# Attention before a mixture of experts: two key blocks of every pair weighted by split products in place of float32 ones, in a new order

## The chip, the cores and the metric

One core of one Trainium2 chip runs the whole kernel. The time is the device time of one execution in microseconds (us), the median of several runs. The engines are named as in the profile: PE (TensorE matmul), PEld (its weight loads), DVE (VectorE), ACT (ScalarE), POOL (GpSimd), SP (SyncE, which issues most DMAs).

## What is computed

Attention with 8 batches of 8 heads, 1152 keys of 64 values each, and queries that are averaged two by two; its output is the input of a layer of 8 experts with a fixed capacity.

```python
q_pool = q.reshape(B, H, S // 2, 2, D).mean(axis=3)            # 8, 8, 576, 64
scores = np.matmul(q_pool, k.transpose(0, 1, 3, 2)) / np.sqrt(D)
attn = np.exp(scores - np.max(scores, axis=-1, keepdims=True))
attn = attn / (np.sum(attn, axis=-1, keepdims=True) + 1e-09)
x = np.matmul(attn, v)                                         # to (4608, 512): one row a token
logits = x @ w_gate                                            # 8 experts
...                                                            # greedy routing, 576 tokens an expert
out[mask] = np.maximum(x[mask] @ w1[e], 0.0) @ w2[e]
```

## The kernel before

**Tiling.** The 64 heads are taken two at a time: 32 *pairs*, numbered 0 to 31. A pair has 18 *steps*, one for each head of the pair and each block of 128 keys (steps 0 to 8 the first head, 9 to 17 the second). A step holds 512 of a head's 576 queries; the 64 queries that are left of either head make the *shared block*, which both heads fill together.

**One step** (`step`, from line 847). PE forms the scores of 128 keys by 512 queries in one of three PSUM banks, by two matmuls of 512 columns (lines 841 and 842). ACT takes the exponential into the float32 tile P (line 858). The high part of P is its upper half, read in place as bfloat16; the low part PM = P - high, in float16, is made by a subtraction (line 863), on POOL, or on DVE for the steps listed in `AT["pd"]` (in pair 0 `AT["pd0"]`) and for two steps of the last pair that are fixed in the code. Then PE multiplies by the values (line 875), twelve matmuls a step: for each 128 queries high by top values, high by low values, low by top values, all added into the one PSUM bank `av`. A step that is listed in `AT["f32"]` is done otherwise: no PM is made, and P is multiplied as float32 by the values in float32 (line 872), which the chip runs as eight instructions a step:

```python
whole = g % NSTEP in AT["f32"]
if not whole:
    en, eng, dur = ("DVE", nc.vector, 600) if g % NSTEP in pd or (n == npair - 1 and g % 3 == 2 and kb > 5) else ("POOL", nc.gpsimd, 1000)
    od.add(g + 0.2, en, dur, lock=1, fn=lambda: eng.tensor_tensor(pm, p, hi, op=OP.subtract), ...)
...
if whole:
    nc.tensor.matmul(a, p[:, qs], VF[:, s, kb], start=False, stop=kb == NKB - 1, skip_group_check=True)
    continue
for y, (out, w, v) in enumerate(((a, hi, top), (a[:, :D], hi, low), (a, pm, top))):
    nc.tensor.matmul(out, w[:, qs], v, ...)
```

**The end of a pair.** The shared block's probabilities PJ are float32 in either kernel, and line 911 multiplies them by the float32 values into the same bank. After that DVE empties `av` (lines 921, 924, 925: RS and X). The products of the next pair cannot begin in `av` before that.

**Work for the next pair** goes on meanwhile: DMAs bring keys, queries and values; ACT and DVE split them into high and low parts (on DVE: KL line 647, QL line 637, the low part of V line 692; each reads two tensors of SBUF); PE forms score maxima in two PSUM banks `mt` (lines 749, 757, 766, 769), DVE reduces them (MX, line 742, then CM line 795), PE turns them (line 818), DVE writes AU (line 820) and frees the bank. Every second pair PE also turns X and forms gate logits (lines 938, 952; LS on DVE).

**Routing tables.** 32 small operations, 22 of DVE and 10 of POOL, build constants for the routing (`routing_tables`, DVE's at line 478). They form one chain, in which each writes what the next one needs.

**The order.** Nothing is scheduled at run time: each engine runs its own list in order. The class `Timed` gives every operation a time: the number of its pair times `PERIOD`, plus its entry in the table `TIME`, whose keys name the pair (0 to 3 by number, `e` and `o` even and odd ones, `y` and `z` the last two), the operation and its step. It then emits the operation with the least time among those whose producers have been emitted. `AT["grp"]` lists after which steps of a head the products that are waiting go out as one group. The experts' part has a planner of its own.

Of the kernel before, what the change touches and what calls it, by code (L numbers as in the profile page):

```python
# [162 lines left out]
class Timed(Order):  # L163
# [21 lines left out]
    def emit(self):  # L185
# [36 lines left out]
      3, "wu": 50, "pd": [], "wv": 65, "pd0": [3, 4, 8, 9, 10, 17], "sp": 0, "d1": 2.5, "cw1":  # L222
      0.5093, "grp": [2, 4, 6, 7, 8, 9],
      "jq": [9, 12, 15], "f32": [16, 17]}
PERIOD = 23600
TIME = {"0auga": 7741, "0augb": 12864, "0augta": 6209, "0augtb": -4893, "0av0a10a": 3692, "0av0a12a": 8723,
# [277 lines left out]
def attention(ctx, tc, top, kb, sx, kt, qt, v, wg, x_dram, L, npair=NPAIR):  # L504
    nc = tc.nc
    const = ctx.enter_context(tc.tile_pool(name="att_const", bufs=1))
    psum = ctx.enter_context(tc.tile_pool(name="att_psum", bufs=1, space=PSUM))
    od = Timed(TIME, PERIOD, npair)

# [1254 lines left out]
```

## Time and profile before

| | |
|---|---|
| runs, median (least to most) | 1263.47 us (1263.2 to 1264.06), 3 runs |
| profiled execution | 1262.77 us, span 1261.0 us, mean granted TensorE clock 0.981 |
| busy PE | 1204.0 us, 95% of the span |
| busy DVE | 942.8 us, 75% |
| busy ACT | 869.3 us, 69% |
| busy POOL | 848.8 us, 67% |

How to read it: attention takes some 763 us of the span, the experts the rest, and the shares are means over both. A matmul's duration in the rows reaches into the next one's, since PE is pipelined; what a matmul costs is read from the distance between starts. The profile's lines are those of the kernel before; in the changed kernel the same code stands three lines higher (872 there is 875 here, 908 there 911 here).

### The profile page before, as it was taken

What the parts mean: (1) busy time and instruction counts of PE and PEld (TensorE: products, weight loads), DVE (VectorE), ACT (ScalarE), POOL (GpSimd) and SP (SyncE); (2) the same over time, 40 slices, a digit from 0 to 9 for tenths busy, and PEclk for the clock granted to TensorE, in tenths of its full rate; (3) what the DMA queues carried; (4) which work ended last, traced back from release to release, by engine and by line L of the source; (5) the groups of instructions that cost most, each with busy time, mean ns of one, the idle gap of its engine ahead of it and who ended that gap; (6) DMA issues with size and microseconds to landing.
All of it is one profiled execution on the core that took longest, in us unless ns stands there. A gap on an engine that the chain in (4) does not pass through costs nothing.

```text
span 1261.0 us, 36741 instructions
## 1 busy us (share of the span) xinstructions
PE 1204.0 (95%) x14619; PEld 839.5 (67%) x14619; DVE 942.8 (75%) x2290; ACT 869.3 (69%) x1603; POOL 848.8 (67%) x882
## 2 busy tenths in 40 slices
PE   8899999999989999999999997799899999999998
PEld 4566666666656666666666675576667677777776
DVE  7898888988887988888898835888776777762320
ACT  6687887888867888888788661457456564667731
POOL 4577787778858768878777680366575756668641
PEclk7899999999989999999999998999899999999999
DMA  7565576566565475566556300432553335253411
GB/s 211 153 170 132 154 178 143 148 166 157 132 150 143 137 174 150 137 163 168 133 148 147 94 10 20 171 127 79 175 168 117 130 118 195 88 196 121 142 38 38
DMA packets 95690, 171.03 MB, mean 136 GB/s; under 512 B 17694, under 2 KB 54558, under 8 KB 93342
## 3 DMA queue, kind: packets, MB, share of 16 engines
q1 hardware_dynamic: 82574, 107.09, 31.8%
q0 software_dynamic: 12800, 61.58, 16.4%
q8 instruction: 115, 1.88, 0.7%
q14 instruction: 57, 0.47, 0.1%
q10 hardware_dynamic: 144, 0.02, 0.0%
HBM read 99.63 MB, written 18.87 MB: 94 GB/s over the span
## 4 chain that ended last, share of the span: by engine, by line
PE 72%; DVE 14%; issue 4%; ACT 3%; POOL 3%; DMA 2%; another core or an unknown queue 0%; SPq 0%; POOLq 0%; DVEq 0%; ACTq 0%
PE po L1681 12%; PE av L875 12%; PE ph L1651 9%; PE sc L841 6%; PE sc L842 6%; DVE MX L742 5%; PE mt L749 5%; PE av L872 5%; PE kb L841 4%; PE kb L842 3%; PE av L911 3%; DVE KL L647 2%; POOL W2L L1635 1%; PE mt L938 1%; PE mt L766 1%
## 5 line engine op out<-in xcount | busy, mean ns | idle before, releaser
L863 POOL TENSOR_TENSOR PM<-P 128x512 f16<-128x512 f32 x506 | 534.6, 1111 | 176.5 <-ACT P L858 173.7
L742 DVE TENSOR_REDUCE MX<-mt 128x2 f32<-128x1024 f32 (+2 forms) x341 | 373.5, 1133 | 42.8 <-PE mt L749 30.1
L858 ACT ACTIVATE P<-sc 128x512 f32<-128x512 f32 x384 | 221.2, 598 | 71.3 <-PE sc L842 61.8
L875 PEld LDWEIGHTS <-P 128*128 128x128 bf16 x4096 | 202.7, 99 | 49.4 <-issue 29.8
L875 PE MATMUL av<-V,P 128*128 128x65 f16 (+1 forms) x4096 | 216.4, 194 | 0.3 <-DVE V L692 0.3
L875 PE MATMUL av<-V,PM 128*128 128x65 f16 x2048 | 209.8, 196 | 0.0
L875 PEld LDWEIGHTS <-PM 128*128 128x128 f16 x2048 | 190.1, 98 | 0.5 <-issue 0.4
L841 PE MATMUL sc<-QA,KA 128*128 128x512 f16 (+1 forms) x768 | 178.5, 286 | 1.1 <-ACT P L858 0.9
L842 PE MATMUL sc<-QB,KB 66*128 66x64 f16 (+2 forms) x768 | 176.6, 286 | 0.0
L1681 PE MATMUL po<-W2H,HX 128*128 128x512 f32 x512 | 169.0, 405 | 0.4 <-DVE OT L1691 0.4
L1651 PE MATMUL ph<-Xh,W1h 128*128 128x320 f16 (+1 forms) x512 | 147.3, 288 | 2.5 <-ACT Xh L1513 1.5
L1651 PE MATMUL ph<-Xl,W1h 128*128 128x320 f16 (+1 forms) x512 | 147.5, 288 | 0.6 <-DVE Xl L1515 0.6
L1651 PE MATMUL ph<-Xh,W1l 128*128 128x320 f16 (+1 forms) x512 | 147.4, 288 | 0.5 <-issue 0.5
L841 PEld LDWEIGHTS <-KA 128*128 128x128 f16 x1152 | 97.7, 99 | 74.4 <-issue 33.6
L858 ACT ACTIVATE P<-kb 128x512 f32<-128x512 f32 x192 | 114.9, 599 | 41.0 <-PE kb L842 40.0
L1660 DVE SCALAR_TENSOR_TENSOR HX<-ph,HX 128x256 fp32r<-128x256 f32 x128 | 53.3, 419 | 102.2 <-ACT HX L1656 98.6
L1681 PE MATMUL po<-W2L,HX 128*128 128x512 f32 (+1 forms) x320 | 127.8, 399 | 0.0
L1635 POOL TENSOR_TENSOR W1l<-W,W1h 128x512 f16<-128x512 f32 x62 | 72.2, 1168 | 77.1 <-ACT W1h L1629 73.3
L1651 PEld LDWEIGHTS <-W1h 128*128 128x128 f16 x1024 | 99.1, 98 | 36.3 <-issue 10.9
L1656 ACT ACTIVATE HX<-ph 128x256 fp32r<-128x256 f32 (+1 forms) x128 | 51.7, 409 | 103.1 <-PE ph L1651 93.6
L842 PEld LDWEIGHTS <-KB 66*128 66x128 f16 (+1 forms) x1152 | 95.2, 98 | 39.0 <-issue 3.3
L1681 PEld LDWEIGHTS po<-W2H,HX 128*128 128x128 f32 x512 | 94.5, 190 | 17.3 <-DVE OT L1691 0.9
(272 smaller groups left out, 2338.8 us busy)
## 6 DMA issues: line engine op xcount, KB each, us to landing
KD<-in_kt_dram SPq DMA_DIRECT2D x64, 288.0 KB
VD<-in_v_dram SPq DMA_DIRECT2D x32, 576.0 KB
QA<-QH SPq DMA_DIRECT2D x128, 72.0 KB
KA<-KH SPq DMA_DIRECT2D x64, 144.0 KB
KB<-KH SPq DMA_DIRECT2D x64, 144.0 KB
KA<-KL SPq DMA_DIRECT2D x64, 144.0 KB
x_dram<-X SPq DMA_DIRECT2D x16, 576.0 KB
QS<-in_qt_dram SPq DMA_DIRECT2D x31, 288.0 KB
```

What stands on the lines that cost most here:

```text
L742: od.add(t, "DVE", d, lambda: nc.vector.tensor_reduce(dst, src, axis=AX.X, op=OP.max), r=[f"m{m}"], w=w, tag="mr", k=z)
L749: nc.tensor.matmul(mt[s][:, y], pairs[b][s], KH[i][h, ks], start=True, stop=True)
L841: nc.tensor.matmul(c, KA[i][:, s, ks], QA[i][:, s, qs], start=first, stop=False, skip_group_check=True)
L842: nc.tensor.matmul(c, KB[i][:kr, s, ks], QB[i][:kr, s, qs], start=False, stop=last, skip_group_check=True)
L858: od.add(g + 0.1, "ACT", 480, lambda: nc.scalar.activation(p, c, AF.Exp, scale=1.0 / UNIT), r=[ck], w=[("P32", g % NP)], tag="exp", k=g % ...
L863: od.add(g + 0.2, en, dur, lock=1, fn=lambda: eng.tensor_tensor(pm, p, hi, op=OP.subtract), r=[("P32", g % NP)], w=[("PM", g % NM)], tag=" ...
L872: nc.tensor.matmul(a, p[:, qs], VF[:, s, kb], start=False, stop=kb == NKB - 1, skip_group_check=True)
L875: nc.tensor.matmul(out, w[:, qs], v, start=kb == 0 and j == 0 and y == 0, stop=kb == NKB - 1 and y == 2, skip_group_check=True)
L1635: eng.tensor_tensor(o, a, b, op=OP.subtract), r=[key] + sr + [(nm + "H", z, y)], w=[(nm + "L", z, y)], first=first, lock=1, tag="wl" if nm ...
L1651: nc.tensor.matmul(p, a[:, d, fs], b[:, d, qs], start=z == 0, stop=z == 11)
L1660: V.scalar_tensor_tensor(HL[:, f, 64 + 256 * hf:320 + 256 * hf], p[:, :256], 0.0, h[:, :256], op0=OP.max, op1=OP.subtract)
L1681: nc.tensor.matmul(o[:n], a[:, z, q0:q0 + n], b[:, z], start=z == 0 and y == 0, stop=z == 7, skip_group_check=True)
```

## The change

The list `f32` becomes empty. Steps 16 and 17 of every pair are done like the others: twelve split matmuls each in place of the float32 ones, and a PM each. The list `pd` gets step 11, whose PM goes from POOL to DVE in pairs 1 to 31. With `grp` the products of a head's steps 6 and 7 go out together. The table `TIME` is new throughout; among its entries the 22 table operations of DVE get times that are 12980 apart.

```diff
-      3, "wu": 50, "pd": [], "wv": 65, "pd0": [3, 4, 8, 9, 10, 17], "sp": 0, "d1": 2.5, "cw1":
-      0.5093, "grp": [2, 4, 6, 7, 8, 9],
-      "jq": [9, 12, 15], "f32": [16, 17]}
+      3, "wu": 50, "pd": [11], "wv": 65, "pd0": [3, 4, 8, 9, 10, 17], "sp": 0, "d1": 2.5, "cw1":
+      0.5093, "grp": [2, 4, 6, 8, 9],
+      "jq": [9, 12, 15], "f32": []}
...
-        "2tablesj": -17424, "2tba": 8188, "2tbb": -15946, "2tbc": -18774, "2tbd": -24432, "2tbe": 311221, "2tbf":
+        "2tablesj": -20403, "2tba": 32600, "2tbb": 45580, "2tbc": 58560, "2tbd": 71540, "2tbe": 84520, "2tbf": 97500,
```

No other line differs, and in the experts' part every engine's list is the same as before. Over the whole kernel POOL makes 537 PMs (506 before) and DVE 39 (6 before).

**PE, the end of pair 20.** P and PM are step tiles, L872 and L911 before are the float32 products of the steps and of the shared block. Before, from the last split product on:

```order
L875 LDWEIGHTS P_134
L875 MATMUL av<-V_99,P_134 128x64
L875 LDWEIGHTS PM_145
L875 MATMUL av<-V_99,PM_145 128x65
L872 MATMUL av<-MS,P_135 128x65 x4
L872 MATMUL av<-MS,P_136 128x65 x4
L841 LDWEIGHTS KA_90
L841 MATMUL sc_153<-QA_94,KA_90 128x512
```

The change, the same place, up to the shared block (L872 is now the split product, L908 the shared block):

```order
L872 LDWEIGHTS PM_147
L872 MATMUL av<-V_99,PM_147 128x65
L872 LDWEIGHTS P_136
L872 MATMUL av<-V_99,P_136 128x65
L872 LDWEIGHTS P_136
L872 MATMUL av<-V_99,P_136 128x64
L872 LDWEIGHTS PM_147
L872 MATMUL av<-V_99,PM_147 128x65
L908 MATMUL av<-MS,PJ 64x65 x18
```

The float32 products of P are gone; the last product before the shared block now reads a PM.

**DVE, the routing tables.** Before, in pair 13's steps, 18 table operations (L478) stand in one piece ahead of AU; the last twelve rows of it:

```order
L478 TENSOR_SCALAR nib<-scratch 128x15 x4
L478 TENSOR_SCALAR nib<-scratch 128x16
L478 TENSOR_SCALAR scratch<-scratch 128x64
L478 TENSOR_SCALAR diag<-scratch 128x64
L478 TENSOR_TENSOR diag<-diag,scratch 128x64
L478 TENSOR_SCALAR scratch<-scratch 128x128
L478 TENSOR_SCALAR same_167<-scratch 128x128
L478 CAST slots<-scratch 128x640
L478 CAST slot_169<-scratch 128x5
L478 TENSOR_SCALAR jval<-scratch 128x36
L478 CAST TAB<-scratch 128x1 x2
L820 TENSOR_SCALAR AU<-mt_157 9x128
```

The change, DVE in one even pair (line 475 is the table operation):

```order
L634 SCALAR_TENSOR_TENSOR QL_88<-QS_119,KS_107,QH_86 128x576
L644 SCALAR_TENSOR_TENSOR KL_85<-KD_114,KS_107,KH_83 128x576
L675 TENSOR_SCALAR VE_125<-mt_156 128x1
L644 SCALAR_TENSOR_TENSOR KL_85<-KD_114,KS_107,KH_83 128x576
L739 TENSOR_REDUCE MX_128<-mt_156 128x2x4
L677 TENSOR_SCALAR VS_113<-VE_125 128x1
L681 TENSOR_SCALAR sx<-VS_113,sx 128x1
L739 TENSOR_REDUCE MX_128<-mt_157 128x2
L953 COPY LS<-mt_156 72x384
L475 TENSOR_TENSOR diag<-diag,scratch 128x64
```

The 22 table operations now stand alone, one or two to a pair, over a dozen pairs.

**DVE, after the first half of `av` is emptied** (X, 128x4x64), even pair. Before:

```order
L925 TENSOR_TENSOR X_104<-av,RS_149 128x4x64
L624 TENSOR_SCALAR KE_110<-KS_108 128x1
L626 TENSOR_SCALAR KE_110<-KS_108,KE_110 128x1
L628 TENSOR_SCALAR KS_108<-KE_110 128x1
L630 TENSOR_SCALAR KS_108<-KS_108 128x1
L742 TENSOR_REDUCE MX_127<-mt_157 128x2
L742 TENSOR_REDUCE MX_127<-mt_156 128x2
L692 SCALAR_TENSOR_TENSOR V_100<-VD_118,VS_113,V_100 128x9x64 x2
```

The change:

```order
L922 TENSOR_TENSOR X_105<-av,RS_149 128x4x64
L627 TENSOR_SCALAR KS_108<-KS_108 128x1
L860 TENSOR_TENSOR PM_141<-P_130 128x512
L689 SCALAR_TENSOR_TENSOR V_100<-VD_118,VS_113,V_100 128x9x64 x2
L739 TENSOR_REDUCE MX_127<-mt_156 128x2
L739 TENSOR_REDUCE MX_127<-mt_157 128x2
L644 SCALAR_TENSOR_TENSOR KL_85<-KD_115,KS_108,KH_84 128x576 x2
```

DVE now makes step 11's PM there, with both V parts straight behind it, and two KL follow after the next two reductions.

## Rows read from the trace of the kernel before

**Rows 1.** Spans: core, us, mean granted TensorE clock.
```profile
core 0: 1261.0 us, clock 0.981
```

**Rows 2.** Timeline, DVE: start us, us, form; start of emptying `av` at pair ends.
```profile
353.37 0.22 DVE L921 TENSOR_SCALAR RS<-av,VS 128x5 f32<-128x5 f32 x1 [2.36 <-PE av L911]
...
383.38 0.22 DVE L921 TENSOR_SCALAR RS<-av,VS 128x5 f32<-128x5 f32 x1
...
405.03 0.22 DVE L921 TENSOR_SCALAR RS<-av,VS 128x5 f32<-128x5 f32 x1 [2.35 <-PE av L911]
...
428.62 0.21 DVE L921 TENSOR_SCALAR RS<-av,VS 128x5 f32<-128x5 f32 x1
...
450.28 0.22 DVE L921 TENSOR_SCALAR RS<-av,VS 128x5 f32<-128x5 f32 x1 [2.36 <-PE av L911]
...
473.72 0.21 DVE L921 TENSOR_SCALAR RS<-av,VS 128x5 f32<-128x5 f32 x1
```

**Rows 3.** Windows: stretch, length, busy PE, PEld, DVE, ACT, POOL (count), clock, DMA.
```profile
366.00:384.00 18.00, 14.19 (x188) 9.94 (x185) 14.45 (x41) 9.30 (x19) 7.16 (x8) 0.81 0.42 102
372.00:374.00 2.00, 1.80 (x19) 0.97 (x19) 1.79 (x8) 0.52 (x1) 0.00 (x0) 0.50 0.04 9
428.60:473.70 45.10, 45.03 (x706) 29.73 (x705) 39.09 (x64) 37.34 (x68) 35.08 (x35) 1.00 0.62 158
722.00:763.00 41.00, 40.77 (x675) 29.29 (x671) 15.05 (x33) 25.01 (x46) 29.53 (x42) 1.00 0.09 24
```

**Rows 4.** Timeline, PE: a split step at 400.21, float32 steps, the shared block.
```profile
400.21 0.22 PE L875 MATMUL av<-V,P 128*128 128x65 f16 x2
...
400.58 0.38 PE L841 MATMUL sc<-QA,KA 128*128 128x512 f16 x1
...
401.88 1.90 PE L872 MATMUL av<-MS,P 128*128 128x65 f32 x16
403.71 1.27 PE L911 MATMUL av<-MS,PJ 128*64 128x65 f32 x36
```

**Rows 5.** Timeline, DVE and then PE, from the first to the last late table operation.
```profile
367.35 0.14 DVE L478 CAST pcole<-scratch 128x1 f32<-128x1 int32 x1
...
368.38 2.04 DVE L478 TENSOR_SCALAR nib<-scratch 128x15 f32<-128x15 int32 x5
...
371.88 0.27 DVE L820 TENSOR_SCALAR AU<-mt 9x128 f16<-9x128 f32 x1
...
372.20 1.01 PE L749 MATMUL mt<-KH,QH 64*128 64x512 f16 x3 [3.81 <-DVE AU L820]
```

**Rows 6.** Groups by form, two pairs (428.6 to 473.7): count, busy us, mean ns, idle before.
```profile
L647 DVE SCALAR_TENSOR_TENSOR KL<-KD,KS,KH 128x576 f16<-128x576 f32 x4 | 4.8, 1231 | 0.0
L692 DVE SCALAR_TENSOR_TENSOR V<-VD,VS,V 128x576 f16<-128x576 f32 x4 | 3.1, 809 | 0.0
L637 DVE SCALAR_TENSOR_TENSOR QL<-QS,KS,QH 128x576 f16<-128x576 f32 x2 | 1.6, 814 | 0.0
L863 POOL TENSOR_TENSOR PM<-P 128x512 f16<-128x512 f32 x33 | 34.7, 1109 | 10.2 <-ACT P L858 9.8
```

**Rows 7.** Timeline, POOL and DVE: five PMs while a KL runs; KL; five PMs alone.
```profile
430.36 5.55 POOL L863 TENSOR_TENSOR PM<-P 128x512 f16<-128x512 f32 x5
...
432.31 1.71 DVE L647 SCALAR_TENSOR_TENSOR KL<-KD,KS,KH 128x576 f16<-128x576 f32 x1
...
462.04 5.03 POOL L863 TENSOR_TENSOR PM<-P 128x512 f16<-128x512 f32 x5
...
469.46 0.81 DVE L647 SCALAR_TENSOR_TENSOR KL<-KD,KS,KH 128x576 f16<-128x576 f32 x1
```

**Rows 8.** Line 863: duration ns least/median/most, first and last start.
```profile
L863 DVE TENSOR_TENSOR PM<-P x6: 679/684/911, 29.3 to 746.8; 128x512 f16<-128x512 f32 x6
```

**Rows 9.** DMA that POOL issues: ns least/median/most.
```profile
L589 POOL DMA_DIRECT2D QS<-in_qt_dram x31: 836/883/1211, 14.2 to 682.8; - x31
```

More of the change, by code (lines that the diff above doesn't have):

```diff
@@ L221 @@
       -3.5, "cw": 0.5093, "fold0": 3.5, "fold1": 13.1, "aug": 13.9, "lag": 3, "np": 10, "nm": 9, "stick": 0.5, "nx":
-      3, "wu": 50, "pd": [], "wv": 65, "pd0": [3, 4, 8, 9, 10, 17], "sp": 0, "d1": 2.5, "cw1":
-      0.5093, "grp": [2, 4, 6, 7, 8, 9],
-      "jq": [9, 12, 15], "f32": [16, 17]}
+      3, "wu": 50, "pd": [11], "wv": 65, "pd0": [3, 4, 8, 9, 10, 17], "sp": 0, "d1": 2.5, "cw1":
+      0.5093, "grp": [2, 4, 6, 8, 9],
+      "jq": [9, 12, 15], "f32": []}
 PERIOD = 23600
-TIME = {"0auga": 7741, "0augb": 12864, "0augta": 6209, "0augtb": -4893, "0av0a10a": 3692, "0av0a12a": 8723,
[125 rows of a table removed]
-        "ekl1a": -26623, "eksa": -30018, "eksb": -103880, "eksc": -115231, "eksd": -117469, "elk0a": -136803, "elk1a":
[13 rows of a table removed]
-        -114263, "evsa": -1138, "evsb": -113652, "evsc": -114069, "evsd": -115770, "exa": -106982, "exb": -112457,
[6 rows of a table removed]
-        -137053, "ofolda": -137487, "ogba": 48053, "ogca": -132261, "ogcb": -129305, "ogla": 47500, "ogma": 46405,
-        "ogpa": -138552, "ogta": 43583, "ogtb": 44271, "ojaa": 38452, "oje0a": -132457, "oje1a": -133851, "oje2a":
-        -135820, "ojq0a": 17219, "ojq1a": 27290, "ojq2a": 33876, "okaa": -47428, "okh0a": -136159, "okh1a": -132399,
-        "okl0a": -31088, "okl1a": -36401, "oksa": -40537, "oksb": -136244, "oksc": -139976, "oksd": -138478, "olk0a":
[14 rows of a table removed]
-        -147762, "ovsd": 3810, "oxa": -128835, "oxb": -134705, "yauga": -318273, "yaugda": -330939, "yaugta": 6464,
[8 rows of a table removed]
-        "yksc": -302753, "yksd": -299894, "ylk0a": -326863, "ylk1a": -324184, "ylpa": -55508, "ylqa": -325577, "ylva":
[13 rows of a table removed]
-        -2194, "yvsb": -303618, "yvsc": -304154, "yvsd": 4358, "yxa": -304843, "yxb": -302503, "zauga": 4408,
[6 rows of a table removed]
-        "zexp9a": -324730, "zfolda": -320551, "zgca": -322303, "zgcb": -322620, "zgcc": -321911, "zgla": -328867,
-        "zglb": -328767, "zglc": -324813, "zgma": -189521, "zgmb": -347199, "zgmc": -348229, "zgta": -205694, "zgtb":
-        -350225, "zgtc": -348229, "zjaa": -176057, "zje0a": -323822, "zje1a": -322054, "zje2a": -326925, "zjq0a":
-        29263, "zjq1a": -216474, "zjq2a": -173800, "zkaa": -65924, "zkh0a": -322199, "zkh1a": -323089, "zkl0a":
-        -36141, "zkl1a": -36407, "zksa": -41417, "zksb": -325815, "zksc": -325806, "zksd": -326595, "zlk0a": -339282,
[14 rows of a table removed]
-        -327483, "zvsc": -331115, "zvsd": -328772, "zxa": -325966, "zxb": -328540}
@@ new lines @@
+TIME = {"0auga": 7900, "0augb": 19260, "0augta": 6495, "0augtb": 5547, "0av0a10a": 10554, "0av0a12a": 11649,
[123 rows of a table added]
+        "ekl1a": -24155, "eksa": -29474, "eksb": -112144, "eksc": -115548, "eksd": -118916, "elk0a": -141449, "elk1a":
[13 rows of a table added]
+        "evl1a": 13524, "evsa": 1884, "evsb": -1627, "evsc": -113184, "evsd": -110115, "exa": 30484, "exb": 38513,
[6 rows of a table added]
+        -156706, "ogca": -73450, "ogcb": -117226, "ogla": 48291, "ogma": 47154, "ogpa": -142314, "ogta": 43792,
+        "ogtb": 44448, "ojaa": 38944, "oje0a": -145530, "oje1a": -136541, "oje2a": -137525, "ojq0a": 16489, "ojq1a":
+        26294, "ojq2a": 33002, "okaa": -43084, "okh0a": -138482, "okh1a": -37150, "okl0a": -34150, "okl1a": -34218,
+        "oksa": -92933, "oksb": -40369, "oksc": -137671, "oksd": -38474, "olk0a": -163407, "olk1a": -165870, "olpa":
[13 rows of a table added]
+        -132343, "ovsc": 78, "ovsd": -139757, "oxa": -135336, "oxb": -135989, "yauga": -303801, "yaugda": -329262,
[8 rows of a table added]
+        "yksd": -319471, "ylk0a": -328886, "ylk1a": -340534, "ylpa": -50002, "ylqa": -329417, "ylva": -329371,
[13 rows of a table added]
+        "yvsc": -301401, "yvsd": -303672, "yxa": -298953, "yxb": -300641, "zauga": -324672, "zaugda": -353869,
[6 rows of a table added]
+        -319452, "zgcb": -327349, "zgcc": -324810, "zgla": -322396, "zglb": -326764, "zglc": -327060, "zgma": -190890,
+        "zgmb": -348791, "zgmc": -348805, "zgta": -297525, "zgtb": -348691, "zgtc": -348648, "zjaa": -283923, "zje0a":
+        -324684, "zje1a": -324324, "zje2a": -324186, "zjq0a": 32954, "zjq1a": -347270, "zjq2a": -290025, "zkaa":
+        -61506, "zkh0a": -321149, "zkh1a": -325421, "zkl0a": -33909, "zkl1a": -9964, "zksa": -325352, "zksb": -323272,
+        "zksc": -40273, "zksd": -329532, "zlk0a": -353918, "zlk1a": -352784, "zlpa": -53128, "zlqa": -351019, "zlva":
[13 rows of a table added]
+        -322479, "zvl1a": -326968, "zvsa": -2519, "zvsb": -327472, "zvsc": -328202, "zvsd": -325582, "zxa": -325054,
+        "zxb": -320417}
```

392 rows, old and new, of the table TIME are left out of this document.

## The prediction

> **What bounds the kernel now.** First I read the spans: one core, 1261.0 us at a mean granted clock of 0.981 [rows 1]. The profiled execution took 1262.77 us, 1.7 us more than its span and 0.7 us less than the median of the runs, 1263.47; the sum below is made against 1262.77, and 0.7 is added at the end.
>
> Then I looked for a period. DVE starts to empty `av` once at the end of each pair, so the distance of these starts is the length of a pair [rows 2]: 21.7 us for one parity (383.38 to 405.03, 428.62 to 450.28) and 23.4 to 23.6 for the other. Two pairs take 45.1. One pair does not fit: 353.37 to 383.38 is 30.0.
>
> The windows say what fills those 45.1 us [rows 3]: PE is busy for 45.03 of them, DVE for 39.1, ACT for 37.3, POOL for 35.1. So in attention PE is the bound, and DVE has only 6 us to spare. Part of that spare time cannot be had, because DVE waits there for the end of a pair: 2.36 us before every second emptying [rows 2]. POOL idles for some 10 us, waiting for ACT's P [rows 6].
>
> **The change, part by part.**
>
> *The products of steps 16 and 17.* Two float32 steps take PE from 401.88 to 403.71, 1.83 us for 16 instructions; the twelve matmuls of one split step take from 400.21 to 400.58, 0.37 us [rows 4]. So a pair saves 1.83 - 2 x 0.37 = 1.09 us of PE, all 32 pairs 34.9 us. Two pairs would need 45.1 - 2.2 = 42.9 us of PE. This is on the bounding engine, so it counts in full until another engine takes over. The regrouping of steps 6 and 7 changes no work, and I cost it at nothing.
>
> *The low parts.* A pair makes two PMs more. POOL gets one of them, net: it makes 17 in place of 16. Five PMs in a row take 5.03 us [rows 7], so one costs 1.0 us of POOL's time. DVE gets step 11's, at 0.68 us [rows 8]. Per two pairs POOL goes from 35.1 to 37.1 and DVE from 39.1 to 40.5. ACT's exponentials are the same in number. POOL's 2 us are covered by its 10 us of idle time; if that cover were gone, each PM that is late would hold back a product of PE, and behind it the last product of the pair, which now needs a PM too (step 17), the emptying of `av`, and so the next pair's products.
>
> *What DVE and POOL do to each other.* This is the uncertain term. KL, QL, the two V parts and DVE's PM each read two tensors in SBUF, and they do not run together with a PM of POOL. One KL beside a busy POOL took 1.71 us, a KL alone 0.81; the five PMs around the first took 5.55 us, five alone 5.03 [rows 7]. So a wait costs DVE up to 0.9 us and POOL 0.5. In two pairs of before there are ten such operations of DVE, and two of them wait: the four KLs take 4.8 us in all, 1231 ns each on average, which is 1.7 us too much, while V and QL stand at 0.81 [rows 6]. Now there are twelve, and POOL is idle not 10 of 45.1 us but some 5 of 43 or 44. The bounds are none waiting (0) and all twelve (12 x 0.9 = 10.8 us). I take four, 3.4 us at 0.85 each: twice as many as now for half the idle time, which is nearer to the rows than either end.
>
> *DVE's sum for two pairs:* 39.1 - 1.7 + 2 x 0.68 + 3.4 is 42.2. The table operations, once spread, lie in about half of these periods and add some 0.3 on average (4.5 us in all, below). To this comes the time in which DVE must wait for PE; it is 6 us now, and I keep 1.2 us of it, about half of the wait ahead of one emptying, since that one is tied to the end of a pair. Together 43.7 us, above PE's 42.9. **So I expect DVE to become the bound, at 43.7 us for two pairs in place of 45.1**. Pairs 2 to 29 are 14 such periods: 14 x 1.4 = **19.6 us** gained.
>
> *The routing tables.* In the pair of 30.0 us, 18 table operations ran on DVE between 367.35 and 371.88, ahead of AU. AU frees a bank of `mt`; a maxima matmul waited for it and PE stood idle for 3.81 us [rows 5]. After that the granted clock was 0.50, the lower of the two levels (1.2 and 2.4 GHz), so the matmuls behind the gap were slower too; over 366 to 384 the mean is 0.81 [rows 3]. Against a pair of the same parity the loss is 30.0 - 23.4 = 6.6 us, gap and clock together. With the operations one or two to a pair no single delay is longer than about 1 us (the costliest five took 2.04 together [rows 5]). I take the whole **6.6 us** as gained; the bounds are 0, if another pile forms, and 6.6. Their own 4.5 us of DVE do not vanish and are in DVE's sum.
>
> *The ends.* In pairs 0 and 1 PE waits for loads and splits, and at the end of attention there are no maxima left to do, and DVE is busy for only 15 of 41 us [rows 3]. At 1.09 us for each of the four pairs 4.4 us could be gained; the order is new there too, and I take half, **2.2 us**, between a loss of 4 and a gain of 4.4. Transfers are the same in number. What SP and POOL issue is moved in their lists, but a transfer for the next pair has most of a pair to land, and the one that POOL issues takes 0.88 us of it [rows 9]; I cost the moves at nothing. The experts' part is unchanged and starts earlier by what attention gains.
>
> *Sum:* 19.6 + 6.6 + 2.2 = 28.4 us; 1262.8 - 28.4 = 1234.4 for a profiled execution, and with the 0.7 **1235 us** for the median.
>
> **A rule against the change.** The rows show a KL costing five PMs of POOL 0.5 us, although the KL's own record is 0.81 long [rows 7]; DVE's side of an operation is not all exclusive. The Trainium skill ("SBUF — State Buffer", section "SBUF: two separate sides") states that DVE and GpSimd share one pair of SBUF ports as an exclusive lock, taken by whichever starts first and held for the whole instruction, with the other fully blocked. The trace agrees that they exclude each other, and has 0.5 us where the whole instruction would be 0.8. What it would do here if it held to the letter is the second rival.
>
> **Rivals.**
>
> 1. *PE stays the bound.* The new order puts DVE's operations where POOL is idle, as all but two in two pairs are now. Then two pairs take 42.9: 14 x 2.2 = 30.8, and with 6.6 and 4.4 the gain is 41.8: 1222 us. For it: PE is busy in 45.03 of 45.1 us [rows 3]. Against it: DVE would need 40.5 or more of 42.9 us with almost no idle time. Chance 0.16.
>
> 2. *The pair of DVE and POOL becomes the bound.* 34 PMs at 1.0, ten DVE operations at 0.81 and two at 0.68 exclude each other: 43.5 us for two pairs; with the two DMAs that POOL issues (0.88 each, [rows 9]) 45.3, if nothing of DVE lies beside those. Halfway, 44.4, the gain is 14 x 0.7 + 6.6 + 1 = 17.4: 1246 us. For it: POOL's idle time shrinks to half. Against it: the 0.5 above. Chance 0.15.
>
> 3. *Only the pile goes.* What PE saves turns into waits of the same length, since the last product of a pair now waits for ACT and POOL, where a float32 step needed ACT alone: two pairs stay at 45.1, the gain is 6.6: 1257 us. Chance 0.05.
>
> 4. *Slower: DVE's waits for POOL take over.* The place is the even pair, where DVE now has eight of the twelve operations: QL and KL, KL, the PM and both V, and twice KL. In such a row each operation after the first lets one PM of a busy POOL go ahead. With eight of twelve waiting (6.8 us) DVE's two pairs are 37.4 + 1.4 + 0.3 + 6.8 + 1.2 = 47.1: 14 x 2.0 = 28 lost, 8.8 gained back by the pile and the ends: 1283 us. It decides from seven on: six (5.1 us) give 45.4, which the 8.8 us outweigh; seven (6.0) give 46.2, a loss of 15.4. For it: POOL nearly always has a PM ready now. Against it: only two of ten wait today. Chance 0.13.
>
> That the change does not do what it says can be left out: the new order has no float32 product of P, and its table operations stand apart.
>
> **How the numbers follow.** My forecast, two pairs at 43.0 to 44.4 us and 1226 to 1245, has 0.46. With rivals 1 to 3 that makes 0.82 for faster by over 0.2% (2.5 us, about what a measurement of this kernel can tell from no change), under 1261. Slower by over 0.2%, above 1266, is rival 4, 0.13. The 0.05 between are two pairs at 45.5 or so, where the gain of the pile is just eaten. The range from 1220 to 1258 holds the forecast, nearly all of rival 1, and rivals 2 and 3, 0.8 together; it leaves out rival 4, the cases of no change and a few that do better than PE's sum.
>
> **What would show it.** Right: no row of float32 products of P, no gap of PE over 3 us and no lower clock around 370; emptyings of `av` 43.0 to 44.4 us apart for two pairs; DVE busy for over 41 us of them; KL, V, QL or DVE's PM with means clearly over 0.81 and 0.68; POOL waiting for P less than half of 9.8 us. Wrong: two pairs at 42.9 or less (the waits were avoided, rival 1); DVE with idle time ahead of the emptying as now; two pairs above 45.1, with long KL rows in the even pairs (rival 4) or with PE waiting for PM; a new pile of table operations, or a second stretch at the lower clock.

## The result and the profile after

The changed kernel takes 1246.51 us, the median of four runs (1246.02 to 1248.98); the kernel before took 1263.34 beside it. The ratio is 0.9877, with a 95% interval of 0.9864 to 0.9891: faster by 16.8 us, where 28.4 were predicted. The profiled execution took 1246.02 us. Line numbers from L586 on are 3 lower than before, so PM is L860, KL L644, V L689, the table operations L475.

First the spans of the changed kernel (core, us, mean granted clock), which answer to [rows 1]:

```profile
core 0: 1243.9 us, clock 0.984
```

Then, as in [rows 2], DVE's timeline at the ends of pairs 11, 12 and 13, and of 18, 19 and 20 (start, us, form, idle time ahead and what ended it):

```profile
303.60 0.22 DVE L918 TENSOR_SCALAR RS<-av,VS 128x5 f32<-128x5 f32 x1 [0.91 <-PE av L908]
...
333.13 0.21 DVE L918 TENSOR_SCALAR RS<-av,VS 128x5 f32<-128x5 f32 x1
...
352.92 0.22 DVE L918 TENSOR_SCALAR RS<-av,VS 128x5 f32<-128x5 f32 x1 [0.64 <-PE av L908]
...
466.40 0.21 DVE L918 TENSOR_SCALAR RS<-av,VS 128x5 f32<-128x5 f32 x1
...
485.81 0.23 DVE L918 TENSOR_SCALAR RS<-av,VS 128x5 f32<-128x5 f32 x1 [0.63 <-PE av L908]
...
510.91 0.21 DVE L918 TENSOR_SCALAR RS<-av,VS 128x5 f32<-128x5 f32 x1
```

Two pairs take 44.5 us here (466.40 to 510.91); the seven periods from pair 16 to 29 have 43.8 to 44.5, 44.2 on average, in place of 45.1. From pair 16 to 25 the odd pairs are shorter (19.4 to 19.8, before 21.65), the even ones longer (24.05 to 25.1, before 23.4 to 23.6). The wait of 2.36 us ahead of an odd pair's emptying has shrunk to 0.63. And one pair does not fit again: 303.60 to 333.13 is 29.5 us. That is pair 12. Pair 14, in whose steps the pile stood before and which took 30.0 us then, now takes 25.2.

The windows answer to [rows 3] (stretch, length, busy PE, PEld, DVE, ACT, POOL with counts, clock, DMA):

```profile
312.00:316.00 4.00, 3.30 (x42) 3.24 (x43) 4.00 (x4) 3.12 (x6) 1.38 (x1) 0.58 0.09 14
416.00:460.30 44.30, 44.12 (x726) 27.98 (x724) 41.34 (x66) 37.53 (x70) 38.89 (x38) 1.00 0.63 159
460.30:504.80 44.50, 43.83 (x722) 27.87 (x721) 41.75 (x66) 37.00 (x69) 38.24 (x37) 1.00 0.60 154
```

DVE is busy for 41.3 to 41.8 us of two pairs (39.1 before), POOL for 38.2 to 38.9 (35.1). In the first of the three stretches the granted clock is 0.58, near the lower of its two levels (1.2 and 2.4 GHz), as behind the pile before.

By form, over 460.3 to 504.8, DVE's operations that [rows 6] and [rows 8] priced, and POOL's (busy us, mean ns, idle time before them):

```profile
L644 DVE SCALAR_TENSOR_TENSOR KL<-KD,KS,KH 128x576 f16<-128x576 f32 x4 | 4.7, 1196 | 0.0
L689 DVE SCALAR_TENSOR_TENSOR V<-VD,VS,V 128x576 f16<-128x576 f32 x4 | 4.1, 1074 | 0.0
...
L860 DVE TENSOR_TENSOR PM<-P 128x512 f16<-128x512 f32 x2 | 2.1, 1064 | 0.0
L634 DVE SCALAR_TENSOR_TENSOR QL<-QS,KS,QH 128x576 f16<-128x576 f32 x2 | 1.9, 938 | 0.0
```

```profile
L860 POOL TENSOR_TENSOR PM<-P 128x512 f16<-128x512 f32 x35 | 38.7, 1179 | 6.3 <-ACT P L855 6.2
```

V, QL and DVE's PM now wait too. Against 809, 814 and 680 ns alone, the twelve operations wait 4 x 0.39 + 4 x 0.27 + 2 x 0.38 + 2 x 0.12 = 3.6 us in two pairs; taken one by one, seven of the twelve wait, for 0.3 to 0.8 us.

In place of the pile of [rows 5] the timeline shows this at the start of pair 12, first DVE, then POOL, then PE:

```profile
304.49 2.35 DVE L739 TENSOR_REDUCE MX<-mt 128x2 f32<-128x1024 f32 x2
306.75 4.00 DVE L475 CAST slots<-scratch 128x640 f16<-128x640 int32 x1
```

```profile
302.50 0.88 POOL L586 DMA_DIRECT2D QS<-in_qt_dram  x1
303.16 7.23 POOL L860 TENSOR_TENSOR PM<-P 128x512 f16<-128x512 f32 x7
```

```profile
312.70 1.54 PE L935 MATMUL mt<-ident,X 128*128 128x128 f32 x6 [3.34 <-DVE MX L739]
```

One table operation, the cast that writes `slots`, took 4.00 us. In the pile of before it had taken 0.48:

```profile
371.19 0.48 DVE L478 CAST slots<-scratch 128x640 f16<-128x640 int32 x1
```

In the changed kernel it ended 0.36 us after POOL's run of seven PMs (310.39). The maxima behind it were late, PE stood idle for 3.34 us and then ran at the lower clock. So the result has three questions: why one cast takes 4 us, what the table operations really give, and why two pairs stop at 44.2.

### The profile page after: what moved, and what is told of

Read it like the earlier page. It is cut to its first block, busy times and chain, and to the rows that moved or that the text cites. A ratio compares the mean times of both kernels' runs of the same rounds, so it can differ in the third digit from the quotient of the medians.

```text
span 1243.9 us, 37266 instructions
## 1 busy us (share of the span) xinstructions
PE 1178.5 (95%) x14875; PEld 808.1 (65%) x14875; DVE 986.0 (79%) x2323; ACT 867.1 (70%) x1603; POOL 897.3 (72%) x913
## 4 chain that ended last, share of the span: by engine, by line
PE 67%; DVE 19%; issue 5%; ACT 3%; DMA 2%; POOL 2%; another core or an unknown queue 0%; SPq 0%; POOLq 0%; DVEq 0%; ACTq 0%
PE av L872 13%; PE po L1678 12%; PE ph L1648 9%; DVE MX L739 6%; PE sc L838 6%; PE sc L839 6%; PE mt L746 5%; PE kb L838 3%; PE kb L839 3%; PE av L908 3%; DVE PM L860 1%; PE mt L935 1%; POOL W2L L1632 1%; DVE V L689 1%; DMA out_dram<-OT,idx 1%
## 5 line engine op out<-in xcount | busy, mean ns | idle before, releaser
L860 POOL TENSOR_TENSOR PM<-P 128x512 f16<-128x512 f32 x537 | 586.1, 1159 | 114.8 <-ACT P L855 105.2
L872 PEld LDWEIGHTS <-P 128*128 128x128 bf16 x4608 | 230.1, 98 | 61.0 <-issue 27.2
L855 ACT ACTIVATE P<-sc 128x512 f32<-128x512 f32 x384 | 224.4, 604 | 44.8 <-PE sc L839 40.5
L872 PE MATMUL av<-V,P 128*128 128x65 f16 (+1 forms) x4608 | 243.6, 193 | 1.1 <-DVE X L922 0.6
L872 PE MATMUL av<-V,PM 128*128 128x65 f16 x2304 | 235.5, 195 | 0.7 <-DVE KS L625 0.5
L872 PEld LDWEIGHTS <-PM 128*128 128x128 f16 x2304 | 212.2, 97 | 1.4 <-DVE PM L860 0.6
L1653 ACT ACTIVATE HX<-ph 128x256 fp32r<-128x256 f32 (+1 forms) x128 | 51.5, 409 | 103.6 <-PE ph L1648 96.0
```

The lines of the kernel that those rows point to most:

```text
L855: od.add(g + 0.1, "ACT", 480, lambda: nc.scalar.activation(p, c, AF.Exp, scale=1.0 / UNIT), r=[ck], w=[("P32", g % NP)], tag="exp", k=g % ...
L872: nc.tensor.matmul(out, w[:, qs], v, start=kb == 0 and j == 0 and y == 0, stop=kb == NKB - 1 and y == 2, skip_group_check=True)
L1653: nc.scalar.activation(HH[:, f, qs], p, AF.Relu)
```

## The experiments

They ran on other chips, where the kernel before takes 1249 to 1251 us. The experts' part takes 485 to 487 us in their traces, in place of 498; undisturbed pairs have the same lengths (23.44 and 21.65 us with the old order and products). So they are compared by their ratios to the kernel before and by the lengths of pairs, which are the distances of the emptyings as above. "2 to 29" is the sum of these pairs. The first two rows are from the chip of the sections before.

```
kernel                     even + odd = two pairs     2 to 29   ratio [95%]
before                     23.44 + 21.65 = 45.1       638.9     1
changed                    44.2 on average            626.7     0.9877 [0.9864, 0.9891]
tables alone               23.44 + 21.65 = 45.1       647.5     1.0069 [1.0051, 1.0087]
tables in clear places     23.44 + 21.65 = 45.1       636.4     0.9987 [0.9977, 0.9996]
new order, float32         23.64 + 21.61 = 45.3       655.9     1.0129 [1.0111, 1.0147]
products, old order        30.3  + 20.9  = 51         715.3     1.0670 [1.0655, 1.0684]
 the same, PMs on POOL     30.6  + 20.9  = 51.5       714.1     1.0627 [1.0612, 1.0641]
slots by two inputs        as changed                 627.6     0.9887 [0.9865, 0.9909]
slots earlier              as changed                 622.3     0.9855 [0.9840, 0.9870]
without one DMA            as changed                 621.6     0.9848 [0.9828, 0.9867]
DVE's PM in odd pairs      24.17 + 19.78 = 43.95      621.8     0.9850 [0.9828, 0.9872]
 and slots earlier         24.18 + 19.79 = 43.97      619.2     0.9836 [0.9818, 0.9853]
all PMs on POOL            24.18 + 19.95 = 44.1       640.8     1.0008 [0.9999, 1.0017]
KL narrow                  22.83 + 20.69 = 43.5       617.4     0.9816 [0.9802, 0.9829]
```

**Why one cast took 4 us.** First the kind of the operation: the same cast as an operation with two inputs.

```diff
-    by(400, V.tensor_copy, C["slots"], it["s"])
+    by(400, V.tensor_tensor, C["slots"], it["s"], it["s"], op=OP.max)
```

> The changed kernel with one table operation of DVE, the cast of 640 whole numbers to float16 (slots), written as the maximum of the tensor with itself: the same values at the same place in the order, but two tensors read in SBUF. In the changed kernel this cast takes 4.0 us while POOL makes seven low parts without a pause, PE stands idle for 3.3 us, and pair 12 takes 29.5 us where its neighbours of the same parity take 24 to 25. Theory: the one-input cast gets the port only when POOL's run has ended, a two-input operation gets in after one low part. Then it takes under 2 us, pair 12 some 25 us, and the kernel 1242 us (4 to 5 less than the changed kernel's 1246.5). Rival: any operation that needs the port waits out the run at that place; then it takes 3 to 4 us again, and the time stays at 1246 to 1247.

It took 4.33 us at the same place, and pair 12 took 29.9, as the rival had it. DVE's timeline:

```profile
308.39 4.33 DVE L475 TENSOR_TENSOR slots<-scratch 128x640 f16<-128x640 int32 x1
```

So one input or two makes no difference to this cast. Next the table operations alone: the kernel before with the table times of the change, all else old.

```diff
-        "2tablesj": -17424, "2tba": 8188, "2tbb": -15946, "2tbc": -18774,
+        "2tablesj": -17424, "2tba": 32600, "2tbb": 45580, "2tbc": 58560,
...
```

> The kernel before with nothing changed but the times of the 22 table operations of DVE, which are those of the changed kernel. Theory: the pile of 4.5 us in pair 14 is gone with its 3.8 us gap of PE and the lower clock behind it, 6.6 us less, and the cast of 640 numbers finds POOL pausing more often than in the changed kernel: 1257 us. Rival: that cast waits for a run of POOL here too and gives back most of it: 1261 to 1263 us, with one pair that is 4 to 6 us long.

Spreading them made the old kernel slower, by 0.7%, which neither the theory nor the rival had; `slots` itself took only 1.35 us. Pair 14 fell to 23.45, so the pile's 6.6 us were gone; but pairs 5, 7 and 11 took 28.0, 24.1 and 27.4. In each a table operation was long: 4.79, 3.05 and 4.86 us. The last one, with POOL beside it, in the two timelines:

```profile
304.87 4.86 DVE L478 TENSOR_SCALAR same<-scratch 128x128 f16<-128x128 int32 x1
```

```profile
304.71 0.88 POOL L589 DMA_DIRECT2D QS<-in_qt_dram  x1
305.30 4.33 POOL L863 TENSOR_TENSOR PM<-P 128x512 f16<-128x512 f32 x4
309.27 1.20 POOL L589 DMA_DIRECT2D QS<-in_qt_dram  x1
```

Here too POOL had issued a DMA, and its PMs followed without a pause. From this came the theory that such a run is closed to DVE until its end. If so, the place decides; the next run moves `slots` to a place ahead of the run.

```diff
-"2tbr": 253260
+"2tbr": 246260
```

> The changed kernel with one number changed: the cast that writes slots (128x640) stands some 7 us earlier on VectorE, behind AU of pair 11 (an odd pair), ahead of the run of PMs that GpSimd makes without a pause from the start of pair 12. Theory (an operation of VectorE that needs the port and falls into a run of PMs behind a DMA that GpSimd issues waits for the end of the whole run; elsewhere it waits for one PM at most): slots takes 0.5 to 1.5 us, pair 12 is 24 to 25 us (29.5 in the changed kernel), nothing else moves, ratio to the kernel before 0.983 (0.9877 in the changed kernel) within 0.002. Rival 1 (the cast itself is long whenever GpSimd works, its place does not matter): slots takes 4 us again, the loss moves to pair 11 or 12, ratio 0.987 to 0.989. Rival 2 (pair 12 is late from something else, and the long cast only fills the wait): slots is short, pair 12 stays at 29, ratio 0.987.

The cast took 0.91 us and pair 12 25.17 in place of 29.53; pairs 2 to 29 gained 4.4 us.

```profile
300.66 0.91 DVE L475 CAST slots<-scratch 128x640 f16<-128x640 int32 x1
```

The ratio missed its expectation: it is 0.9855. In this profiled execution pair 1 took 26.65 us, in the changed kernel 24.21, with the same order there: PE waited 0.9 us for a DMA (`QB`), and the granted clock was 0.94 there, not 1.00. Why the DMA was late is open. The decisive run leaves the place alone and takes the DMA away (pair 15 lacks the low part of its queries).

```diff
-            od.add(t + 2, "POOL", 1000, lambda: nc.gpsimd.dma_start(...
+            n == 15 or od.add(t + 2, "POOL", 1000, lambda: nc.gpsimd.dma_start(...
```

> The changed kernel without one DMA: the accumulating transfer that GpSimd issues at the start of pair 12 (the low part of pair 15's queries, at 302.50 us in the changed kernel's trace) is left out, so pair 15 is computed without that part. The slots cast stays where it took 4.00 us. Theory (the PMs close up into a run without a gap only behind a DMA that GpSimd issues): the PMs there keep their 1.04 us each, slots takes at most 1.5 us, pair 12 is 24 to 25.5 us in place of 29.5, the other pairs as in the changed kernel. Rival (a run of ready PMs is enough, the DMA has no part in it): slots takes 4 us or more, pair 12 stays above 28.

The cast took 0.78 us and pair 12 24.31. DVE's timeline, and below it the PMs' durations as min/median/max ns: of this kernel from 306 to 311 us, then of the changed kernel in its run.

```profile
309.77 0.78 DVE L475 CAST slots<-scratch 128x640 f16<-128x640 int32 x1
```

```profile
L860 POOL TENSOR_TENSOR PM<-P x5: 1036/1038/1286, 306.2 to 310.2; 128x512 f16<-128x512 f32 x5
```

```profile
L860 POOL TENSOR_TENSOR PM<-P x7: 1240/1264/1291, 303.2 to 309.2; 128x512 f16<-128x512 f32 x7
```

For this cast the cause is shown: the place and the PMs that are ready are the same, only the DMA is gone. The PMs start 1.00 us apart in both. Without the DMA ahead of them each takes 1.04 us and the next begins 0.04 before its end; the cast got in at the first end, though three more PMs followed without a gap. Behind the DMA each takes 1.26, the next begins 0.26 before its end, and the cast waited for the end of the run, through four PMs.

**What the table operations are worth.** The kernel before again with the table operations spread, the three long ones moved out of the runs (the edit is against the run with the tables alone).

```diff
-"2tbf": 97500, ..., "2tbj": 149420, ..., "2tbq": 240280, ...
+"2tbf": 92500, ..., "2tbj": 158420, ..., "2tbq": 252280, ...
```

> The kernel before with the table operations at the changed kernel's places, as in the run with the tables alone, but the three that took 3 to 4.9 us there (pcol's second cast, one of nib's, same) each put at a place outside the run of PMs that follows GpSimd's DMA in the odd pairs. Theory (the place decides): each of the three takes under 1.1 us, pairs 5, 7 and 11 are back at 21.5 to 22, pair 14 stays at 23.5, so that all 6.6 us of the pile are gained: ratio 0.9948 within 0.0015. Rival (spread out, the table operations cost as much as in a pile, wherever they stand): 6 us or more come back in other pairs, ratio 1.000 or above.

The three took 0.73, 0.79 and 0.85 us, pair 14 stayed at 23.45, and no long operation was left. Yet 2 to 29 gained 2.5 us, not 6.6: against the kernel before, pairs 5, 7 and 13 are 0.65 longer, 8 and 10 some 0.5, pair 12 1.8. The ratio, 0.9987, lies between the theory and its rival. So 4 of the 6.6 us come back in small pieces. PE shows where: in pairs 5, 7 and 13 it now waits 0.7 us for DVE's VE, and in pair 12 0.8 us for a reduction of maxima, which it did in none of them before (us in total, times, longest; pairs 13 and 12):

```profile
PE mt L757 <- DVE VE L678: 0.7, 1, 0.7
...
PE mt L952 <- DVE MX L742: 0.8, 1, 0.8
```

**The order and the products, each without the other.** The change with its float32 products back, and no PM on DVE:

```diff
-"pd": [11], ..., "f32": []
+"pd": [], ..., "f32": [16, 17]
```

> The changed kernel's order, table times and groups with the float32 products of steps 16 and 17 back, and no low part on DVE beyond pair 0 and the last pair. Theory (the split products give the gain, the order carries it): PE again needs 45.1 us for two pairs, the pile is gone, 1257 to 1262 us, depending on the cast of 640 numbers. Rival (the order alone gives the gain): 1246 us or less.

Two pairs take 45.3 us, as before, and pairs 5, 11 and 12 take 28.0, 28.0 and 29.6, with table operations of 4.5, 4.6 and 3.5 us in the runs. The whole is slower than the theory and the rival had it (1.0129). The new order by itself gives the steady pairs nothing. The other half is the products with the old table of times:

```diff
-"pd": [], ..., "grp": [2, 4, 6, 7, 8, 9], ..., "f32": [16, 17]
+"pd": [11], ..., "grp": [2, 4, 6, 8, 9], ..., "f32": []
```

> The kernel before with the products of the change alone: steps 16 and 17 as split products with their low parts, step 11's PM on VectorE, the regrouped steps; every other instruction keeps the old table of times, so the table operations stand in one pile in pair 14. Theory (the split products give the gain of the steady pairs, the new order mainly spreads the table operations, which gains about 2.5 us where they stand well): two pairs 43.9 to 44.8 us outside pair 14, pair 14 still 5 to 7 us long, ratio 0.985 to 0.992. Rival (without the new order, operations of VectorE fall into the runs of PMs behind GpSimd's DMAs, which are longer now): two pairs above 45.1, with V or KL or QL rows of 2 us and more, ratio above 1.

Two pairs take 51 us: slower, as the rival had it, but not by its mechanism: no V, KL or QL of the steady pairs is longer than 1.7 us. PE waits for PMs, in two pairs 2.7 us for DVE's, which stands behind two maxima and both V parts, and 2.6 for one of POOL's. So the PM was taken from DVE (the edit is against this run):

```diff
-"pd": [11]
+"pd": []
```

> The run before it without VectorE's PM: the kernel before with steps 16 and 17 as split products, the regrouped steps and all 18 PMs of a pair on GpSimd (the two new ones where the table of times puts them); VectorE's order in the steady pairs is the old one, pile included. Theory (the run before it was slow only because VectorE's PM stood behind V in the old order, where TensorE waited 4.1 us for it): two pairs 43.9 to 44.8 us outside pair 14, pair 14 5 to 7 us longer than its neighbours of the same parity, ratio 0.985 to 0.993. Rival (the old order does not fit 36 PMs on GpSimd either, and the new order is a part of the steady pairs' gain): two pairs above 45.1, with TensorE waiting for a PM of GpSimd or with KL, V or QL rows of 2 us and more, ratio above 1.

The theory fell: 51.5 us, with PE waiting for PMs of POOL, as the rival had it. The waits of PE over two pairs, 524.3 to 575.8 (us in total, times, longest), and the window, columns as above:

```profile
PE av L875 <- POOL PM L863: 6.2, 2, 3.7
PE mt L757 <- DVE VE L678: 0.4, 1, 0.4
```

```profile
524.30:575.80 51.50, 44.66 (x722) 28.91 (x721) 41.73 (x64) 37.30 (x68) 41.43 (x39) 0.93 0.54 135
```

PE waits 6.2 us for two PMs of POOL, and the clock falls to 0.93 on average. Both waits lie in the even pair, and the timelines of POOL and PE show where the first comes from:

```profile
561.43 8.11 POOL L863 TENSOR_TENSOR PM<-P 128x512 f16<-128x512 f32 x6 [3.37 <-ACT P L858]
```

```profile
563.53 0.20 PE L875 MATMUL av<-V,PM 128*128 128x65 f16 x1 [2.59 <-POOL PM L863]
```

In an even pair POOL's list in this kernel makes the PMs of steps 13, 12, 10, 16, 9, 14, 17, 11, 15, in this order. So the new PM, of step 16, stands ahead of step 9's. POOL stood idle until ACT had made step 16's P, though step 9's P had been ready for 12 us, and PE waited for step 9's PM. The second wait, 3.66 us, is for step 11's PM, behind the other new one, of step 17; here DVE's V, KL and QL lie beside POOL, and each PM takes 1.55 to 1.58 us, not 1.04. In the run with DVE's PM step 16 stands ahead of step 9 just the same. The old table has times for the PMs of steps 16 and 17, but the kernel before makes no such PM, so these times had never ordered anything in it. As they were run, neither half of the change is faster, and together they are. That the old order could not carry the split products is not shown: the two new PMs at better places in it were not tried.

**Why two pairs stop at 44.2.** Four runs take work from DVE. The first leaves DVE its PM in odd pairs alone:

```diff
-        pd = AT["pd" if n else "pd0"]
+        pd = AT["pd0"] if not n else AT["pd"] if n % 2 else []
```

> The changed kernel with step 11's low part on DVE in odd pairs alone; in the 15 even pairs from 2 to 30 POOL makes it. Theory: DVE bounds the even pairs (24 to 25 us each, odd ones 19.4 to 19.8), where its low part takes 1.06 us with its wait; without it they are about 1 us shorter, 14 us in all: 1232 us. Rival: POOL is the bound there (one low part more in the even pairs costs it 1.0 us): no gain or a loss, 1246 to 1255 us.

It gained 4.9 us over the changed kernel in pairs 2 to 29, 1.9 of them in pair 12, less than expected. From pair 14 to 24 every even pair is now 24.2; those of 25.1 there are gone. With `slots` earlier as well:

```diff
-"2tbr": 253260
+"2tbr": 246260
-        pd = AT["pd" if n else "pd0"]
+        pd = AT["pd0"] if not n else AT["pd"] if n % 2 else []
```

> The kernel with the earlier slots cast, and VectorE makes its PM of step 11 in the odd pairs alone (in the even pairs GpSimd makes it). If the two gains add: even pairs 24.2 and odd 19.8 us as in the run that had the odd PM alone, pair 12 at 24 to 25, ratio 0.980 within 0.002, the fastest so far. Rival (the odd PM's gain was in pair 12 alone, where the run of PMs lay differently): ratio as with the earlier slots cast alone, 0.983.

Two pairs 43.97, pair 12 24.19, 2 to 29 at 619.2, ratio 0.9836: faster than both kernels. The lengths of the pairs are those of the theory, the ratio is that of the rival; pair 1 took 26.65 us here too. Next all of DVE's PMs go to POOL:

```diff
-"pd": [11]
+"pd": []
```

> The changed kernel with VectorE's one PM a pair given to GpSimd: VectorE does some 2.1 us less in two pairs, GpSimd 2 times 1.1 us more. Theory (VectorE with its waits for the port paces two pairs: 41.75 us of work in 44.5, GpSimd 38.2): two pairs fall to 43 to 43.7 us, ratio 0.979 to 0.984. Rival (GpSimd paces, or TensorE's 43.8 does): two pairs 44.2 to 45, ratio 0.988 to 0.995, with GpSimd at 40 us or more in two pairs.

Two pairs 44.1, near the rival's 44.2, with POOL busy for 40.4; the ratio, 1.0008, is above both. POOL's runs of PMs are longer now, and six table operations fall into them (2.4 to 5.6 us), which eats all of the gain. Last, KL for 64 of 576 columns:

```diff
-            od.add(t + 5 + 2 * z, "DVE", 727, lock=1, fn=lambda h=h: nc.vector.scalar_tensor_tensor(
+            od.add(t + 5 + 2 * z, "DVE", 727, lock=1, fn=lambda h=slice(z * M, z * M + (M if n < 2 else 64)): nc.vector.scalar_tensor_tensor(
```

> The changed kernel with VectorE's low parts of the keys, KL, made for 64 of 576 columns of each half from pair 2 on (so the scores lack part of their low terms): the same number of instructions on every engine in the same order, VectorE about 4 us less in two pairs, with their waits. Theory (in steady pairs VectorE's work and its waits for the port take back what TensorE saved): two pairs fall from 44.3 to between 42.9 and 43.6 us, ratio 0.968 to 0.980. Rival (another chain holds the pairs, as when GpSimd took the PM of VectorE and two pairs stayed at 44.1): two pairs stay at 43.9 to 44.2, ratio 0.982 to 0.988, pair 12 as before.

Two pairs take 43.5 us; the ratio is short of the theory's, since `slots` still costs pair 12 (28.4). The windows of two pairs: this kernel, then the one with the odd PM and the earlier cast.

```profile
434.00:477.60 43.60, 43.47 (x725) 27.78 (x725) 38.77 (x66) 37.01 (x69) 37.80 (x37) 1.00 0.64 161
```

```profile
437.40:481.40 44.00, 43.62 (x723) 27.73 (x721) 41.15 (x65) 37.06 (x69) 40.07 (x38) 1.00 0.62 158
```

With DVE at 38.8 us two pairs are 0.7 shorter than on average in the changed kernel, not more. PE's busy time hides its short waits, as the ends of matmuls are modelled; the distances from one start to the next show them. Summed by kind over pairs 16 to 23, per two pairs, us:

```
                              before   changed   KL narrow
float32 products of P           3.64      0         0
split products of P            11.87     13.61     13.60
maxima (mt<-KH,QH)              4.96      5.84      5.17
scores (sc and kb)             19.19     19.27     19.17
two pairs                      45.13     44.34     43.57
```

Each distance is counted to the kind that it starts with. The products save 3.64 - 1.74 = 1.90 us. 0.88 of that is lost between one maxima matmul and the next, which wait for DVE to read the banks; with less work on DVE that falls to 0.21. Without such losses two pairs would take 45.13 - 1.90 = 43.2 us, so at 43.57, with KL narrow, little is left for DVE to hold back.

## Why the prediction was right or wrong

The total was right within its range of 1220 to 1258, but 1246.5 lies outside the narrower forecast of 1226 to 1245, and 16.8 us are well under the 28.4 of the sum. The mechanism was right for the most part, one term was too large and one failed. Of its signs, PE's gap of over 3 us with the lower clock behind it came back, at another place, and POOL waits 6.2 us for P, not less than half of 9.8.

*The split products* were to save 2.2 us of PE in two pairs; the steps show 1.90. The rule by which it was worked out holds, the twelve matmuls of a step being a little dearer (13.61 - 11.87 for 48 of them, 0.43 a step, not 0.37).

*DVE's waits for POOL* were the uncertain term: 3.4 us taken, between 0 and 10.8; the rows give 3.6. That the sum fits is partly luck: four operations were to wait for 0.85 us each, and seven wait for 0.5 on average. All four kinds now stand above their times alone.

*DVE's sum* came to 43.7 us for two pairs; 44.2 were measured. DVE's busy time was near (42.5 with the table operations, measured 41.3 to 41.8), but in one period it still idles for 2.75 us of 44.5, where 1.2 were kept. "DVE becomes the bound" is half right: PE loses 0.88 us to it, but with DVE relieved by some 3 us two pairs still take 43.5. The fourteen periods gained 14 x 0.87 = 12.2 us (45.1 to 44.23), not 19.6.

*The routing tables* are the step that failed: "no single delay is longer than about 1 us", hence 6.6 us gained. The five rows that it took for the costliest are those of `nib`; the longest of them took 1.08 us and `slots` 0.48, each where it stood in the pile. The pile is gone, but one operation fell into a closed run. Pairs 2 to 29 take 7.5 us more than 14 x 44.23 in the changed kernel, and they took 7.5 more than 14 x 45.1 before: the term is zero. The bound "0, if another pile forms" was the right end, for another reason: not a pile, but one cast at a bad place, 4.4 us of pair 12 by the run that moved it. And even in good places, in the old kernel, the spread operations gave 2.5 of 6.6.

*The ends* were put at 2.2; pairs 0, 1, 30 and 31 gained 4.6. Pairs 30 and 31 gave 2.06. Pair 0 ended between 54.1 and 60.7 us in the profiled executions, so the rest should not be read closely, and that this term makes up for a part of the others is luck.

Together 12.2 + 0 + 4.6 = 16.8, which is 1262.8 - 1246.0.

*The rivals.* The first, PE at 42.9, did not come. The second named 1246 us, by its price for the port, but not by what happened: POOL still waits 6.2 us of 44.5 for P, and with 35 or 36 PMs on POOL in place of 34 two pairs did not get longer (43.97 and 44.1). The third is out. The fourth, slower through DVE's waits in the even pairs, has its sign from the odd and even lengths (even pairs are up to 1.7 us longer), and those of 25.1 went with DVE's PM there; but it was far from deciding: seven operations waited, from which number on it was to decide, but for 3.6 us in all where it counted 6.0. The runs with the old order showed another way to lose: PE waiting for PMs that stand in a bad place, behind the new ones in POOL's list or on DVE behind V, 5.3 and 6.2 us in two pairs and the clock behind it, with DVE's long operations as a part of it.

## What to carry to other kernels

Before an operation that shares a port with another engine is moved into a busy stretch, look at what that engine does there: not only how long one of its operations is, but whether they follow each other without a gap, and whether a DMA that it issues stands at the head of the row. New work needs a place in each engine's order: an operation that is not ready holds up all that stand behind it in the list. Spreading a pile of small operations is worth less than the gap that the pile makes: spread out, they still delay what stands behind them on their engine, even where that engine has idle time over the whole pair.

## What was not expected of the hardware

Behind a DMA that POOL issued (0.87 us), PMs that were ready took 1.24 to 1.36 us each and overlapped, the first by 0.21 to 0.29 with the DMA, and a table operation of DVE that arrived then mostly waited for the last of the run. In seven kernels (the changed one, the cast with two inputs, the tables alone, the new order with float32, all PMs on POOL, DVE's PM in odd pairs, KL narrow) eighteen table operations took over 1.5 us, up to 5.56; each of them began in such a run with a DMA at its head, and ended with the run's last PM or up to 0.7 us after it. In all fourteen traces no row of PMs overlaps like this without a DMA at its head. Not every operation waits: the fill of `nib` and casts of one column into `TAB` that began in such runs took 0.12 to 0.13 us. With the DMA left out the same PMs took 1.04 us and the same cast 0.78. The Trainium skill ("SBUF — State Buffer", section "SBUF: two separate sides") states that the one that starts first holds the shared port pair for the whole instruction. By that the cast would have waited for one PM, some 1.3 us at most (an estimate from these rows); here it waited for four, so the measurement goes further than the rule. Why a DMA issue lets the following operations overlap more is open.
